# RWKV attention feeding a tanh-shrink MLP: two thirds of x @ w_in in blocks 6 to 11 as seven 128-column products, summed on VectorE

## The chip, the cores and the metric

The kernel runs on one core of one Trainium2 chip. The time is the device time of one execution in microseconds. The engines are named as the profile names them: PE (TensorE, with its weight loads as PEld), DVE (VectorE), ACT (ScalarE), POOL (GpSimd) and SP (SyncE, which only issues transfers). Everything is float32.

## The reference

```
def _attn_ref(r, k, v, w, u):              # r, k, v: (4, 8, 768, 48)
    for t in range(S):
        cur = einsum('bhd,bhe->bhde', u * k[t], v[t])
        y[t] = einsum('bhd,bhde->bhe', r[t], state + cur)
        state = w * state + einsum('bhd,bhe->bhde', k[t], v[t])
def _moe_ref(x, w_in, w_out):              # (3072, 384), (384, 2048), (2048, 384)
    h = x @ w_in
    g = h - tanh(h)
    return g @ w_out
```

The attention's output, laid out as 3072 tokens of 384, is x.

## The kernel before

**Tiling.** The 3072 tokens are 12 blocks of 256 (j = 0 to 11). The attention of a block is two units of 64 time steps and two batch rows each, 24 units in all; a unit ends with x transposed (384 channels on partitions in three slices of 128, kk = 0, 1, 2), written by ACT (`to_xt`, `to_rest`) and, for the channels that lie on the wrong partitions, by six small transfers that POOL issues (`fill`). d_ff is cut into 8 tiles of 256 columns. One block with one such tile is a tile of the MLP, T*j*.*n*: 96 in all. Blocks 0 to 5 go through d_ff in three passes (`PASSES`: tiles 0 and 1, then 2 and 3, then 4 to 7, each pass over all six blocks), blocks 6 to 11 in one.

**A tile.** `h` makes the 256 x 256 tile of x @ w_in transposed: two halves of 128 columns of d_ff, each three matmuls of 128 x 256 over the slices kk. A float32 matmul stands in the profile as two records, so this is 12 records. Then ACT reads h in PSUM three times (`s`, `th`, `tg`) and works on its own results twice (`sq`, `small`). DVE makes g = h - th (with h in PSUM), m (tg = s * tg) and copies m over g where the argument is small (`cp`, for the accuracy of h - tanh(h) near zero). Then POOL makes three sums of quarters of g (`sums_of_g`: one of 128x256, two of 128x128; on DVE for the last tiles of block 11), and PE the product with w_out (`products`), which is already done as seven products of 128 x 192 for eight, in two parts of 8 and 6 records, into four PSUM banks `p`. `mix` prepares the sums of w_out that it needs, on DVE, while blocks 2 to 5 run. At a block's end ACT and DVE put the four banks together (`collect`, and `gather` where an earlier pass left sums in `parts`), and POOL issues the stores. The last tile of block 11 has its product with w_out done plainly (`o`, `ALONE = 2`).

**What sets the order.** Nothing is scheduled while the program is built. `lay_out` lists all tasks with what they wait for, and `ORDER`, a string of task numbers, gives the order in which `written` emits them; each engine runs its own tasks in that order, and a wait stalls everything behind it on its engine. The costs and due times in the `add` calls are not used in this kernel. A PSUM tile named `h` is one of two buffers, so the h of a tile waits until s, th, tg and g of the tile two before have read theirs. g is one of five buffers and waits for the products of the tile five before. xt is one of eight buffers (`FIRST + 2`), reused after eight blocks.

Of the kernel before, what the change touches and what calls it, by code (L numbers as in the profile page):

```python
# [10 lines left out]
F32 = mybir.dt.float32  # L11
# [17 lines left out]
C = 128  # L29
# [10 lines left out]
EASED = 12  # L40

# [4 lines left out]
    "00010K2j2k2l2g2h2i0I2n2m2obXbX020F0L030J040605bXbY2r3536372p3332340A0G2t0B0C2s2vbXbY2y072w2z082x2u0U092+0M390N3V"  # L46
    "3D2_2q0O383A3B3H303W3X0P3F0V3I3T3J3C3K3E3S3U3G0Q3LbXbXbY3M0W3v3c310T3NbY3d3w3x0R3O3b3g3t3P3h3Q3s3u3f0S3Z3R3ibY8E"
    "0x3e3j0X3l3Y3a403k0Y4Q440Z8F0e3m4P4R0a454M41468G4N4O3n0b473z0D0c3_3o0E0d433p42bZ8Q160f483y3+3q4q0g8I494a4p4r0h4W"
    "4b0i4A4m8J4cbZ4B4S0j4d4n4o4X3r4C4V0k4T4U8R4w0m4D4Y5J4Z4K4E4e8M4L5Hba4f4J0l5K5L8S4G8H5G5I4g4I8K4H8Lba4v8T144h4+8V"
# [4 lines left out]
    "9L7M7b9M6v9U7j9V7k0H7D0y9K7F6wKM9e7GKNKO0z907a7c7e9f6x9NKPKR9W736y9C7H701M9Z7l6+717N0+K26_729g9D7O9X9i9a7d9Y7f9j"
    "Kt9b7P7mKv17KAK3K49O7QKBKwKx6z9P7h7gKsKu7RKaKb9s0_7SKS189h107n9R9Q9k9l9c197o111A7p129t7q9m1U1V1F9d1G7r1B1H7wA29n"
    "7u9w1C7v1I7yA31D7x9v7z9u9o9zA51f1gKC1W9x1X1J1hKD1i9pLG1KA6LHLIAG9y1N9q1OA4AHA91P9+9rAS9_KEA7ATA8AAAKKcA0AJABAVAN"
    "A11QKd1RACAI1SALAgAM1TAUAh1jAWAOAXAZAYAD1kAEAa1lAsK7AFAbLJAiAtKXAj1yAPAlLKLLAkAQLm1mAnLnLoAoARAvAwAuAzB4Ax1nAmB5"
# [1232 lines left out]
```

## Time and profile before

| | us |
|---|---|
| time, median of 3 runs (lowest, highest) | 579.02 (577.75, 583.08) |
| the profiled execution's own time | 576.89 |
| its span, first to last instruction | 575.2 |
| last h of block 11 ends on PE (start of the run of `p` that follows) | 556.85 |
| last instruction of DVE | 571.05 to 571.60 |

| tiles and units | engine | busy us of the span | share |
|---|---|---|---|
| all | PE | 562.6 | 98% |
| all | PE's weight loads | 481.1 | 84% |
| all | DVE | 430.3 | 75% |
| all | ACT | 404.3 | 70% |
| all | POOL | 202.8 | 35% |

The page gives per group of instructions the line, the engine, the shapes (partitions x elements), the count, the busy time and the mean of one in ns. In a view along the time each row has the start, the length, the engine and the line; a group of equal instructions is one row, with its count. Windows give the busy time of PE, PEld, DVE, ACT and POOL in a stretch, in that order, each with its number of records.

### The profile page before, as it was taken

How to read it: one execution, taken by the hardware profiler on the slowest of the kernel's cores; microseconds unless marked ns; L12 is line 12 of the kernel's file. 1: busy time of each engine (PE TensorE's matmuls, PEld its weight loads, DVE VectorE, ACT ScalarE, POOL GpSimd, SP SyncE). 2: the span in 40 equal slices, each digit the busy share in tenths (PEclk: the TensorE clock that was granted, in tenths of full speed). 3: DMA queues.
4: the chain of work that ended last, by engine and by line, in shares of the span. 5: the costliest groups of instructions: out<-in, count | busy, mean ns of one | idle time of the engine just before them, and what ended most of it. 6: DMA issues, size and time to landing. Idle time of an engine off the chain costs nothing.

```text
span 575.2 us, 14185 instructions
## 1 busy us (share of the span) xinstructions
PE 562.6 (98%) x5495; PEld 481.1 (84%) x5495; DVE 430.3 (75%) x720; ACT 404.3 (70%) x927; POOL 202.8 (35%) x366
## 2 busy tenths in 40 slices
PE   7989999999999999999999999999999999999997
PEld 4667777777677789999899899999999898999995
DVE  5899977989998877776897987487685774564445
ACT  2799999998778565545884875766785668666461
POOL 5101221300000236353345455182454263654430
PEclk9999999999999999999999999999999999999999
DMA  8987686535730000032344452442123010010011
GB/s 131 175 200 133 115 178 147 109 68 141 157 91 0 1 1 21 8 56 42 45 75 84 65 92 43 74 85 37 25 51 60 17 34 6 5 29 2 0 29 30
DMA packets 138399, 38.23 MB, mean 66 GB/s; under 512 B 130744, under 2 KB 132760, under 8 KB 138328
## 3 DMA queue, kind: packets, MB, share of 16 engines
q1 hardware_dynamic: 129996, 29.52, 28.5%
q0 software_dynamic: 4992, 6.99, 5.3%
q10 hardware_dynamic: 3340, 0.79, 0.9%
q8 instruction: 44, 0.72, 0.6%
q14 instruction: 27, 0.22, 0.1%
HBM read 31.46 MB, written 4.72 MB: 63 GB/s over the span
## 4 chain that ended last, share of the span: by engine, by line
PE 80%; DMA 1%; ACT 1%; POOL 0%; DVE 0%; issue 0%; POOLq 0%
PE h L217 39%; PE p L307 28%; PE o L254 7%; PE yk_ps L614 5%; DMA xt<-rest 1%; PE p L254 0%; ACT xt L773 0%; POOL xt L794 0%; ACT rest L773 0%; ACT st L188 0%; DVE last L265 0%; DVE state L800 0%; PE x_ps L614 0%; ACT kT L700 0%; POOLq L171 0%
## 5 line engine op out<-in xcount | busy, mean ns | idle before, releaser
L217 PE MATMUL h<-xt,w_in_sb 128*128 128x256 f32 x1152 | 269.0, 381 | 1.0 <-DVE w_in_sb L191 0.7
L217 PEld LDWEIGHTS h<-xt,w_in_sb 128*128 128x128 f32 x1152 | 214.8, 190 | 33.7 <-DVE w_in_sb L191 1.3
L290 POOL TENSOR_TENSOR sg<-g 128x256 f32<-128x256 f32 x69 | 56.9, 826 | 200.1 <-DVE g L246 145.6
L242 DVE TENSOR_TENSOR g<-h,th 128x512 f32<-128x512 f32 x96 | 65.8, 687 | 61.0 <-ACT tg L233 20.1
L244 DVE TENSOR_TENSOR tg<-s,tg 128x512 f32<-128x512 f32 x96 | 71.3, 746 | 32.9 <-ACT s L224 29.4
L229 ACT ACTIVATE s<-h 128x512 f32<-128x512 f32 x96 | 57.1, 595 | 54.1 <-PE h L217 39.5
L307 PE MATMUL p<-mixed,sg 128*128 128x192 f32 x426 | 93.0, 327 | 0.0
L246 DVE COPY_PREDICATED g<-small,tg 128x512 f32<-128x512 int32 x96 | 73.8, 778 | 12.6 <-ACT small L235 9.9
L231 ACT ACTIVATE th<-h 128x512 f32<-128x512 f32 x96 | 56.9, 594 | 35.0 <-PE h L217 34.7
L307 PEld LDWEIGHTS p<-mixed,sg 128*128 128x128 f32 x426 | 73.6, 190 | 1.4
L233 ACT ACTIVATE tg<-h 128x512 f32<-128x512 f32 x96 | 56.6, 592 | 22.9 <-DVE g L246 13.6
L307 PE MATMUL p<-w_out_sb,g 128*128 128x192 f32 x284 | 69.9, 328 | 0.0
L235 ACT ACTIVATE small<-s,smallb 128x512 f32<-128x512 f32 x96 | 68.5, 721 | 1.2
L254 PE MATMUL o<-w_out_sb,g 128*128 128x384 f32 x192 | 67.2, 489 | 0.1
L224 ACT ACTIVATE s<-s 128x512 f32<-128x512 f32 x96 | 60.1, 630 | 1.1
L794 POOL DMA_DIRECT2D xt<-rest x66 | 32.6, 498 | 66.2 <-ACT rest L773 65.4
L307 PEld LDWEIGHTS p<-w_out_sb,g 128*128 128x128 f32 x284 | 51.1, 190 | 2.7
L254 PEld LDWEIGHTS o<-w_out_sb,g 128*128 128x128 f32 x192 | 35.9, 190 | 19.4 <-issue 0.2
L712 ACT ACTIVATE at<-same,du 128x64 f32<-128x64 f32 x184 | 47.7, 339 | 3.9 <-DVE du L708 3.6
L292 POOL TENSOR_TENSOR sg<-sg,g 128x128 f32<-128x128 f32 x69 | 39.7, 579 | 3.6
L294 POOL TENSOR_TENSOR sg<-sg,g 128x128 f32<-128x128 f32 x69 | 37.7, 553 | 3.0
L307 PE MATMUL p<-w_out_sb,sg 128*128 128x192 f32 x142 | 34.8, 327 | 0.0
(130 smaller groups left out, 652.2 us busy)
## 6 DMA issues: line engine op xcount, KB each, us to landing
st<-in_moe_w_out_dram SPq DMA_DIRECT2D x8, 768.0 KB, 5.3
st<-in_moe_w_in_dram SPq DMA_DIRECT2D x16, 288.0 KB, 5.3
rt<-in_r_dram SPq DMA_DIRECT2D x46, 96.0 KB, 3.4
vt<-in_v_dram SPq DMA_DIRECT2D x46, 96.0 KB, 3.1
kt<-in_k_dram SPq DMA_DIRECT2D x44, 96.0 KB, 3.1
out_dram<-o POOLq DMA_DIRECT2D x44, 96.0 KB, 2.1
st<-in_moe_w_in_dram POOLq DMA_DIRECT2D x16, 96.0 KB, 6.0
parts<-in_k_dram SPq DMA_DIRECT2D x48, 32.0 KB, 2.0
```

The costliest lines, as they stand in the source:

```text
L217: self.nc.tensor.matmul(t.h2[:, z], self.w_in_sb[:, t.f // 2, kk, z * 128 : (z + 1) * 128], self.xts[t.j][:, kk].rearrange("p b t -> p (b ...
L224: A.activation(t.s, t.s, AF.Square, scale=G3)
L229: A.activation(out, t.h, AF.Arctan, scale=G2)
L231: A.activation(out, t.h, AF.Tanh)
L233: A.activation(out, t.h, AF.Tanh, scale=G1)
L235: A.activation(out, t.s, AF.Relu, bias=self.smallb, scale=-1.0)
L242: V.tensor_tensor(t.g, t.h, t.th, ALU.subtract)
L244: V.tensor_tensor(t.tg, t.s, t.tg, ALU.mult)
L246: V.copy_predicated(t.g, t.small.bitcast(I32), t.tg)
L254: self.nc.tensor.matmul(self.outs[i], t.g2[:, z, i * C : (i + 1) * C], self.w_out_sb[:, t.f + z, :], start=t.first and z == 0, stop=t.last ...
L290: add(t.s4[:, :2], g[:, 0::3], g[:, 1:2].to_broadcast([128, 2, C]), ALU.add)
L307: self.nc.tensor.matmul(ps[bank][:, half * n : (half + 1) * n], a, b, start=t.first and half == 0, stop=t.last, skip_group_check=True)
```

## The change

For blocks 6 to 11, all tiles but the last two of block 11 (`PLAIN = 4`), 46 tiles, the slices kk = 0 and 1 of x @ w_in are treated as a 2 x 2 by 2 x 2 product of 128 x 128 pieces and made with seven products for eight; the slice kk = 2 stays plain, as four products of the same size. `h_products` issues these 11 matmuls of 128 columns (22 records) in two parts: part 0, four matmuls into one buffer `h` (`ha`), part 1, seven into another (`hb`). So a tile takes both buffers, and each part waits for the reader of the part of the same kind one tile before.

`h_sums` puts h together in SBUF, in the tile of g: ACT copies one 128x128 quarter of `ha`, and DVE adds four times (128x256, 128x256, 128x128, 128x256), each with one operand in PSUM and one in SBUF. The first add reads `ha`, the other three `hb`. s, th, tg and g read h in SBUF after that; so g = h - th has both operands in SBUF. `g`'s buffer is taken by the ACT copy and not by the subtraction, so the wait for the products of the tile five before moves to that copy.

The sums of w_in (`mix_w`, twelve instructions, eight of 128x3x128 and four of 128x2x128) and of x (`mix_x`, four for each of the blocks 6 to 11, one of 128x256 and three of 128x128) are made by POOL. The first two sets of `mix_w` write over the slots of x of blocks 0 to 3 and wait for the last h of blocks 0 and 1, and of 2 and 3; the third writes into `parts` and waits for the gathers of blocks 3 to 5. `mix_x` waits for the block's fills and for the last h of the block two before (for block 6 and 7: gathers).

x no longer has eight rotating buffers but one array `held` of eight slots; blocks 8 to 11 use the slots of blocks 4 to 7 and wait for those blocks' last h.

`ORDER` is another string from its 458th task on: PE's order is the same until the second pass of block 5, at about 190 us.

```diff
+PLAIN = 4
-    "00010K2j2k2l2g2h2i0I2n2m2obXbX020F0L030J040605bXbY2r3536372p3332340A0G2t0B0C2s2vbXbY2y072w2z082x2u0U092+0M390N3V"
+    "00010K2j2k2l2g2h2i0I2n2m2ofhfh020F0L030J040605fhfi2r3536372p3332340A0G2t0B0C2s2vfhfi2y072w2z082x2u0U092+0M390N3V"
...
+    def h_products(self, t, part):
+
+        bank = self.ps_d.tile([128, 4, C], F32, name="h", tag="h")
+        setattr(t, "hb" if part else "ha", bank)
+        f, x = t.f // 2, self.xts[t.j]
+        w = self.w_in_sb[:, f].rearrange("p k (m t) -> p k m t", m=2)
+        a, b = self.mixed_w(f), self.mixed_x[t.j]
+        of = [[(2, w[:, 0, 0], x[:, 0, 0]), (1, a[:, 1], b[:, 2]), (0, w[:, 1, 0], x[:, 1, 0]), (0, w[:, 2, 0], x[:, 2, 0])],
+              [(0, a[:, 0], b[:, 0]), (1, a[:, 2], b[:, 3]), (1, w[:, 2, 1], x[:, 2, 1]), (2, a[:, 3], x[:, 1, 1]),
+               (2, w[:, 2, 0], x[:, 2, 1]), (3, w[:, 1, 1], b[:, 4]), (3, w[:, 2, 1], b[:, 1])]][part]
+        for n, (at, left, right) in enumerate(of):
+            self.nc.tensor.matmul(bank[:, at], left, right, start=n == 0, stop=n == len(of) - 1 or of[n + 1][0] != at,
+                                  skip_group_check=True)
+    def h_sums(self, t, n):
+
+        V = self.nc.vector
+        if n == 0:
+            t.g2 = self.gpool.tile([128, 2, self.d.NT], F32, name="g", tag="g")
+            t.h = t.g = t.g2.rearrange("p z t -> p (z t)")
+        q = t.g.rearrange("p (a t) -> p a t", a=4)
+        if n == 0:
+            self.nc.scalar.copy(q[:, 1], t.ha[:, 2])
+        elif n == 1:
+            V.tensor_tensor(q[:, 0::3], t.ha[:, :2], q[:, 1:2].to_broadcast([128, 2, C]), ALU.add)
+        elif n == 2:
+            V.tensor_tensor(q[:, 1:3], t.hb[:, :2], q[:, 3:4].to_broadcast([128, 2, C]), ALU.add)
+        elif n == 3:
+            V.tensor_tensor(q[:, 3], t.hb[:, 0], q[:, 2], ALU.add)
+        else:
+            V.tensor_tensor(q[:, 1:3], t.hb[:, 2:], q[:, 1:3], ALU.add)
+    def mix_w(self, f, x):
...
+        self.nc.gpsimd.tensor_tensor(s[:, :, out], a, b, op)
+    def mix_x(self, j, n):
...
+        self.nc.gpsimd.tensor_tensor(out, left, right, ALU.subtract)
-            t.g2 = self.gpool.tile([128, 2, self.d.NT], F32, name="g", tag="g")
-            t.g = t.g2.rearrange("p z t -> p (z t)")
+            if not hasattr(t, "ha"):
+                t.g2 = self.gpool.tile([128, 2, self.d.NT], F32, name="g", tag="g")
+                t.g = t.g2.rearrange("p z t -> p (z t)")
+    held = const.tile([128, FIRST + 2, NK, L, C], F32, name="held", tag="held")
...
+            for f, free in ((slice(0, 3), [last_h[0], last_h[1]]), (slice(3, 6), [last_h[2], last_h[3]]),
+                            (slice(6, 8), sum((gathered[j] for j in (3, 4, 5)), []))):
...
+                now = add("PE", .89, lambda: dense.h_products(t, 0), [x_ready[j], mixed_f[f // 2], b1.h] + before, due, steps=16)
+                x.made = add("ACT", .25, lambda: dense.h_sums(t, 0), [now, b5.o, b1.made])
+                first = add("DVE", .33, lambda: dense.h_sums(t, 1), [x.made])
+                users += [x.made, first]
+                before, users = bank(), h_users[-1]
+                x.h = add("PE", 1.55, lambda: dense.h_products(t, 1), [now] + before, due + 1.3, steps=28)
+                sums = [first]
+                for n in (2, 3, 4):
+                    sums.append(add("DVE", .2 if n == 3 else .33, lambda n=n: dense.h_sums(t, n), [x.h, sums[-1]]))
```

Three places in the order. In the rows, L343, L345 and L347 are the three sums of g in the changed kernel (L290, L292 and L294 before), L398 and L345 the stores after and before, L866 and L794 the fills, L264 is `mix_w`, L271 `mix_x`, L237 `h_products`, L222 a plain h (L217 before), L360 and L307 the products with w_out; `p_...` are its four banks.

First place: POOL while block 3 is in its third pass. Before, from the first sum of tile T3.4:

```order
L290 TENSOR_TENSOR sg<-g 128x256
L294 TENSOR_TENSOR sg<-sg,g 128x128
L292 TENSOR_TENSOR sg<-sg,g 128x128
L294 TENSOR_TENSOR sg<-sg,g 128x128
L345 DMA out_dram<-o 64x384
L290 TENSOR_TENSOR sg<-g 128x256
L292 TENSOR_TENSOR sg<-sg,g 128x128
L294 TENSOR_TENSOR sg<-sg,g 128x128
```

After, from the first `mix_w` of the second set, which waits for the last h of T3.7:

```order
L264 TENSOR_TENSOR held<-w_in_sb 128x3x128
L343 TENSOR_TENSOR sg<-g 128x256 x2
L345 TENSOR_TENSOR sg<-sg,g 128x128
L347 TENSOR_TENSOR sg<-sg,g 128x128
L264 TENSOR_TENSOR held<-held,w_in_sb 128x3x128
L343 TENSOR_TENSOR sg<-g 128x256
L264 TENSOR_TENSOR held<-w_in_sb 128x3x128
L398 DMA out_dram<-o 64x384 x2
L345 TENSOR_TENSOR sg<-sg,g 128x128
L347 TENSOR_TENSOR sg<-sg,g 128x128
L345 TENSOR_TENSOR sg<-sg,g 128x128
L347 TENSOR_TENSOR sg<-sg,g 128x128
```

Three sums of w_in now stand ahead of the last sums of g of T3.5 and T3.6 (the last four rows), and behind a wait for PE.

Second place: the first h of block 6, on PE. Before, the end of unit 14's outputs (`yk_ps`), products, and the h of T6.0 with the first half of the next (nine matmuls in one row); unit 13, which completes x of block 6, is further ahead, before the products of T4.6:

```order
L614 MATMUL yk_ps<-vt_123,kw_117 64x48 x16
L307 MATMUL p_2543<-mixed,sg 128x192
L307 MATMUL p_2541<-mixed,sg 128x192
L307 MATMUL p_2544<-w_out_sb,sg 128x192
L307 MATMUL p_2541<-w_out_sb,g 128x192
L307 MATMUL p_2542<-mixed,g 128x192
L307 MATMUL p_2543<-w_out_sb,g 128x192
L307 MATMUL p_2542<-mixed,sg 128x192
L217 MATMUL h<-xt,w_in_sb 128x256 x9
```

After, the last products of T4.7 and the two parts of T6.0:

```order
L360 MATMUL p_2447<-mixed,sg 128x192
L360 MATMUL p_2448<-w_out_sb,g 128x192
L360 MATMUL p_2448<-mixed,sg 128x192
L360 MATMUL p_2449<-w_out_sb,sg 128x192
L237 MATMUL h<-held,w_in_sb 128x128
L237 MATMUL h<-parts,held 128x128
L237 MATMUL h<-held,w_in_sb 128x128 x2
L237 MATMUL h<-parts,held 128x128 x2
L237 MATMUL h<-held,w_in_sb 128x128
L237 MATMUL h<-held 128x128
L237 MATMUL h<-held,w_in_sb 128x128
L237 MATMUL h<-parts,w_in_sb 128x128 x2
```

And on POOL the six fills of block 6 with what stands between them and that h:

```order
L866 DMA held<-rest 16x256 x6
L398 DMA out_dram<-o 64x384 x2
L343 TENSOR_TENSOR sg<-g 128x256
L345 TENSOR_TENSOR sg<-sg,g 128x128
L271 TENSOR_TENSOR parts<-held 128x256
L271 TENSOR_TENSOR parts<-held,parts 128x128
L271 TENSOR_TENSOR parts<-held 128x128
L271 TENSOR_TENSOR parts<-held,parts 128x128
```

The fills are now followed by four sums of x, for which the first h of the block waits. On PE, between unit 13's outputs and T6.0 stand the products of T4.5, T4.6 and T4.7 and the plain h of T5.7, and nothing else.

Third place: DVE in block 6. Before, in the collecting of a block (L335) beside the attention of a unit:

```order
L242 TENSOR_TENSOR g<-h,th 128x512
L688 STREAM_TRANSPOSE kT<-parts 128x512
L689 TENSOR_TENSOR kT<-kT,inverse 128x512
L335 TENSOR_TENSOR o<-u,p_2543 128x192
L815 TENSOR_TENSOR kw_118<-kt,w_down 128x8x48
L244 TENSOR_TENSOR tg<-s,tg 128x512
L246 COPY_PREDICATED g<-small,tg 128x512
L244 TENSOR_TENSOR tg<-s,tg 128x512
```

After (L250 to L256 are the four adds of `h_sums`, L297 is m, L299 cp, L388 the collecting, L392 the gather):

```order
L250 TENSOR_TENSOR g<-h,g 128x2x128
L388 TENSOR_TENSOR u<-e,p_2447 128x192
L388 TENSOR_TENSOR o<-u,p_2447 128x192
L388 TENSOR_TENSOR o<-u,p_2448 128x192
L388 TENSOR_TENSOR o<-e,p_2448 128x384
L392 TENSOR_TENSOR o<-o,parts 128x384
L388 TENSOR_TENSOR o<-o,p_2449 128x192
L252 TENSOR_TENSOR g<-h,g 128x256
L297 TENSOR_TENSOR tg<-s,tg 128x512
L392 TENSOR_TENSOR o<-o,parts 128x384
L254 TENSOR_TENSOR g<-h,g 128x128
L299 COPY_PREDICATED g<-small,tg 128x512
```

The adds of one tile stand between the instructions of the tiles before it; the first add of a tile frees its buffer `ha`, the last its buffer `hb`, for the PE's next tile.

More of the change, by code (lines that the diff above doesn't have):

```diff
@@ L90 @@
+    "eLe2eKeJeMdUdVeYepdWe4e3eNe5dodpdqe6e7e8dAd8dXdYdrdse9eAeOeZeaePeQeTd7eReSeUebeeedeseqecehefegeiejereteuevexewf7"
+    "f8fTfUeyfAf9fBe_ezf0e+f1f2f3fEfCf4fXfVfDfFfGfHfIfJfYfWfZfbfafcekenelemd9eof5f6fKfLfMfNfdfOfPfQfRfSfefgff"
 )
@@ L780, in given, with xt_at @@
                         copy(out[i * PAD : (i + 1) * PAD, z], y[to(i, z), i])
+            def xt_at(j):
+                return j if j < FIRST + 2 else j - 4
             def to_xt():
                 if slot == 0:
-                    dense.xts[j] = work.tile([128, NK, L, C], F32, name="xt", tag="xt", bufs=FIRST + 2)
+                    dense.xts[j] = held[:, xt_at(j)]
                 given(dense.xts[j][:, :, slot].rearrange("e p (z t) -> e z p t", z=2), y_ps[:, :, :NK])
@@ L840, in unit @@
                               [x.cp, x.diag, x.v, b1.xt, b1.rest, b1.add] + ([x.extra] if direct else [x.kw]), steps=96 if direct else 128)
-            x.xt = add("ACT", 1.2 if swap else .4, to_xt, [now, last_h.get(j - FIRST - 2) if slot == 0 else None])
+            x.xt = add("ACT", 1.2 if swap else .4, to_xt, [now, last_h[j - 4] if slot == 0 and j >= FIRST + 2 else None])
             if direct:
@@ L855, in lay_out, with by_seven, mixing_w, mixing_x @@
         tiles, stored, gathered = [], {}, {}
-        mixed = []
+        mixed, mixed_f, x_ready, h_users = [], {}, {}, []
+        def by_seven(j, f):
+            return j >= FIRST and not (j == d.NB - 1 and f >= d.NF - PLAIN)
+        def mixing_w():
+            plan.at = "mixing w"
+            for f, free in ((slice(0, 3), [last_h[0], last_h[1]]), (slice(3, 6), [last_h[2], last_h[3]]),
+                            (slice(6, 8), sum((gathered[j] for j in (3, 4, 5)), []))):
+                now = None
+                for x in range(4):
+                    now = add("POOL", .68 if f.stop == 8 else .95, lambda f=f, x=x: dense.mix_w(f, x), [now] + free)
+                for n in range(f.start, f.stop):
+                    mixed_f[n] = now
+        def mixing_x(j):
+            plan.at = "mixing x", j
+            now, ready = None, filled[j, "all"] + (gathered[j - 3 if j == FIRST else j - 2] if j < FIRST + 2 else [last_h[j - 2]])
+            for n in range(4):
+                now = add("POOL", .68 if n == 0 else .41, lambda n=n: dense.mix_x(j, n), [now] + ready)
+            x_ready[j] = now
         def mixing():
@@ L953, in lay_out @@
             done += part
-        for n in range(early, d.NU):
-            unit(n)
+        mixing_w()
         for j in range(FIRST, d.NB):
+            for n in range(len(units), min(L * (j + 4), d.NU)):
+                unit(n)
             ends = (d.NF,) if j < d.NB - 1 else (d.NF - ALONE, d.NF)
```

133 lines of the change are left out of this document (85 added, 48 removed).

## The prediction, as put on record before the changed kernel ran

> **What bounds the kernel now.** I read the page first, then PE's waits, then the chain in order of time.
>
> ```profile
> span 575.2 us, 14185 instructions
> PE 562.6 (98%) x5495; PEld 481.1 (84%) x5495; DVE 430.3 (75%) x720; ACT 404.3 (70%) x927; POOL 202.8 (35%) x366
> PE 80%; DMA 1%; ACT 1%; POOL 0%; DVE 0%; issue 0%; POOLq 0%
> L217 PE MATMUL h<-xt,w_in_sb 128*128 128x256 f32 x1152 | 269.0, 381 | 1.0 <-DVE w_in_sb L191 0.7
> ```
>
> PE is busy 98% and holds 80% of the chain that ended last; the x @ w_in group (L217) alone has 269 us and waited 1.0 us. The next rows are PE's only wait between 105 and 571 us, and the busy times of blocks 6 to 9 (columns: PE, PEld, DVE, ACT, POOL, then clock, transfers).
>
> ```profile
> PE h L217 <- DMA xt<-rest: 0.3, 1, 0.3
> 311.00:485.00 174.00, 174.00 (x1898) 158.33 (x1897) 126.41 (x211) 120.05 (x292) 79.91 (x134) 1.00 0.30 50
> ```
>
> The reader is to see that PE has no gap in these 174 us, at a granted clock of 1.00, and DVE has 174 - 126.4 = 47.6 us to spare. So fewer PE records shorten the kernel, one for one, as long as DVE, POOL and ACT deliver what PE waits for.
>
> The profiled execution took 576.89 us: span 575.2 and 1.7 around it. That is 2.1 us below the median, 579.02. I make the sum on the span and put the difference on the median.
>
> **PE: 22 short records for 12 long ones.**
>
> ```profile
> 121.51 2.59 PE h L217 x12
> 214.29 2.28 PE p L307 x14
> 15.08 0.60 PE L664 MATMUL x_ps<-ident,rt 128*128 128x128 f32 x4
> L664 PE MATMUL x_ps<-ident,rt 128*128 128x128 f32 x48 | 7.5, 280 | 1.7 <-DMA rt<-in_r_dram 1.3 <-DVE at L838 0.3
> 16.22 0.30 PEld L542 LDWEIGHTS h<-ident 128*128 128x128 f32 x2
> L217 PEld LDWEIGHTS h<-xt,w_in_sb 128*128 128x128 f32 x1152 | 214.8, 190 | 33.7 <-DVE w_in_sb L191 1.3
> ```
>
> The first two are rows of the chain: a tile's h is 12 records of 256 columns in 2.59 us, 0.216 each; a product with w_out is 14 of 192 in 2.28, 0.163 each. Both are 0.85 ns per column, each with a weight load of its own. At 128 columns that gives 0.109. The question is whether a load fits into 0.109. One load takes 0.19, but the row of two takes 0.30, so the next starts 0.11 after the first. And four 128-column matmuls with a load each (transposes) take 0.60; less one record's own 0.28 (the mean of their group) that is (0.60 - 0.28) / 3 = 0.11. I take 0.11: a tile 22 x 0.11 = 2.42 for 2.59, -0.17 us, and for 46 tiles **-7.6 us**. The ends: 0.109 gives -8.1; if records kept the 0.163 of the nearest plain products, 46 x (3.59 - 2.59) = +46. The gain is gone at 2.59 / 22 = 0.118. The evidence for 0.11 is short bursts near the start, hence a rival below.
>
> The Trainium skill (TensorE: Matmul & The Clock Gate, "Back-to-back issue gap") speaks against this change: in a stream of load and matmul pairs a 128-column matmul takes about 81 ns against 56 alone, so loads bind. Its ratio, 1.45, on 0.109 would make an estimated 0.158 per record, 3.48 per tile and +41 us. The transposes at 0.11 do not show it.
>
> **POOL in block 3's third pass.** Eight `mix_w` of three slices move into POOL's row there, of which three (with two stores) stand ahead of the sums of g of T3.5 and T3.6, behind a wait for T3.7's h.
>
> ```profile
> L290 POOL TENSOR_TENSOR sg<-g 128x256 f32<-128x256 f32 x69 | 56.9, 826 | 200.1 <-DVE g L246 145.6
> L292 POOL TENSOR_TENSOR sg<-sg,g 128x128 f32<-128x128 f32 x69 | 39.7, 579 | 3.6
> L294 POOL TENSOR_TENSOR sg<-sg,g 128x128 f32<-128x128 f32 x69 | 37.7, 553 | 3.0
> L345 POOL DMA_DIRECT2D out_dram<-o x44 | 24.1, 548 | 25.7 <-DVE o L339 19.1 <-DVE o L335 6.4
> ```
>
> Sums of 128 elements cost 0.57, of 256 0.83, so 384 are about 1.08. Between T3.7's h and the last sum of T3.5 the order gives POOL three `mix_w`, 3 x 1.08, three sums of 256, 3 x 0.83, six of 128, 6 x 0.57, and two stores, 2 x 0.55: 10.2 us. PE in that time has the h of T4.4 and T4.5 (5.18), T3.4's product (2.28) and the first half of T3.5's (1.30): 8.76. The second half waits about **+1.4**, and all of PE behind it. Bounds: 0, if POOL catches part of its sums beside DVE's waits, and +2.5, if two of its sums meet DVE as below (1.14 for 0.83, and more). The other `mix_w`, and the third set of four smaller ones, fall where POOL is often idle (200 us in all before L290); I cost them at nothing.
>
> **The first h of block 6.** It now waits for six fills and then four `mix_x`.
>
> ```profile
> 294.82 0.63 PE L614 MATMUL yk_ps<-vt,kw 64*64 64x48 f32 x32
> 311.04 2.32 PE L217 MATMUL h<-xt,w_in_sb 128*128 128x256 f32 x10
> 297.12 1.33 ACT L773 ACTIVATE xt<-yk_ps 64x192 f32<-64x192 f32 x4
> 298.46 0.91 ACT L773 ACTIVATE rest<-yk_ps 64x64 f32<-64x64 f32 x4
> 302.77 1.49 POOL L794 DMA_DIRECT2D xt<-rest  x3
> xt<-rest POOLq DMA_DIRECT2D x66, 16.0 KB, 2.2
> ```
>
> Before, 15.6 us lay between unit 13's outputs and that h. Now the order leaves PE three products and one plain h between: 3 x 2.28 + 2.59 = 9.43. The path: ACT 1.33 + 0.91, six fills 6 x 0.50 = 3.0, the landing 2.2 (stores and sums of g run meanwhile), `mix_x` 0.83 + 3 x 0.57 = 2.5, hand-offs 0.4: 10.4. PE waits **+1.0**; bounds 0 (ACT and fills overlap) and +2.5 (ACT starts 1.7 late, as in the rows above). Later blocks' fills come many tiles ahead; I cost their `mix_x` (24 us of POOL over 150) at nothing. The landing of a fill now matters there as it did at the 0.3 us wait above.
>
> **DVE in blocks 6 to 9.** This is the largest unknown. Per tile four adds: three of 256 elements, one of 128.
>
> ```profile
> L290 DVE TENSOR_TENSOR sg<-g 128x256 f32<-128x256 f32 x2 | 0.7, 413 | 0.0
> L292 DVE TENSOR_TENSOR sg<-sg,g 128x128 f32<-128x128 f32 x2 | 0.6, 283 | 0.0
> 222.08 0.34 DVE L335 TENSOR_TENSOR u<-e,p 128x192 f32<-128x192 f32 x1
> 222.45 0.35 DVE L335 TENSOR_TENSOR o<-u,p 128x192 f32<-128x192 f32 x1
> 204.51 0.55 DVE L267 TENSOR_TENSOR parts<-o,parts 128x384 f32<-128x384 f32 x1
> 204.98 0.55 DVE L316 TENSOR_TENSOR mixed<-mixed,w_out_sb 128x384 f32<-128x384 f32 x1
> ```
>
> Independent instructions start 0.08 before the last ends; one that needs the last starts 0.03 after (222.08 + 0.34 to 222.45). So a tile adds between 3 x 0.33 + 0.20 = 1.2 and 3 x 0.44 + 0.31 = 1.6 us. 32 tiles: 38 to 52 us, on 126.4 makes 165 to 179. PE's own time shrinks to 174 - 32 x 0.17 = 168.7. DVE is as full as PE, and whatever it has beyond PE's time, or loses in waits, PE loses too: 0 to +10.
>
> A second cost: g = h - th reads h in PSUM today and two tiles in SBUF after.
>
> ```profile
> 205.44 0.68 DVE L244 TENSOR_TENSOR tg<-s,tg 128x512 f32<-128x512 f32 x1
> 209.67 1.22 DVE L244 TENSOR_TENSOR tg<-s,tg 128x512 f32<-128x512 f32 x1
> 209.19 1.14 POOL L290 TENSOR_TENSOR sg<-g 128x256 f32<-128x256 f32 x1 [5.54 <-PE p L307]
> L242 DVE TENSOR_TENSOR g<-h,th 128x512 f32<-128x512 f32 x96 | 65.8, 687 | 61.0 <-ACT tg L233 20.1
> L244 DVE TENSOR_TENSOR tg<-s,tg 128x512 f32<-128x512 f32 x96 | 71.3, 746 | 32.9 <-ACT s L224 29.4
> ```
>
> m (L244, both inputs in SBUF) takes 0.68 alone and 1.22 beside a POOL sum; its mean is 0.746, that of g (one input in PSUM) 0.687. So g becomes like m: 32 x 0.06 = +1.9 us of DVE. The Trainium skill (SBUF, State Buffer, "Who interferes with whom") says the same of a DVE instruction with two SBUF inputs; the rows above agree.
>
> Where does PE then wait? Its next part 1 needs the three adds from `hb`, 0.33 + 0.20 + 0.33 and three hand-offs of 0.03: 0.95 us. Meanwhile PE makes the next part 0, 8 x 0.11 = 0.88, and one product, 2.28: 3.16. Alone on DVE the adds leave 2.2 to spare; behind a pair m and cp (0.68 + 0.76) still 0.8. Where a block is collected the order puts between a tile's first and last add the collecting, m, a gather and cp: about 5 x 0.35 + 2 x 0.55 + 0.75 + 0.55 + 0.76 = 4.9, with the adds 5.8, against 3.16 with one product or 5.44 with two beside it. That is a wait of 0.4 to 2.6, once per block; four blocks end in this stretch. I take 1.0 each, nearer the lower end because products often stand in pairs in PE's order: **+4**, a third of the 0 to +12 by the sums above. In blocks 10 and 11 DVE has no attention left, and I take nothing there but the tail.
>
> **Moved waits.** g's buffer is now taken by ACT's copy, some 2 us earlier than by g.
>
> ```profile
> DVE g L242 <- PE p L307: 6.7, 3, 3.5
> L326 ACT COPY e<-p 128x192 f32<-128x192 f32 x12 | 3.8, 314 | 6.8 <-PE p L307 6.8
> ```
>
> g waited three times for products, 6.7 us in all, which cost PE nothing; now s, th and tg of earlier tiles queue behind such a wait on ACT. Bounds 0 and 3 x 2 = +6 if all three fell into blocks 6 to 11 and PE starved for each; I take 0, since PE's products stand ahead of what ACT would feed. The copies are 46 x 0.31 = 14 us at most, on an ACT that is 70% busy: off the path. Slots of x that come back after four blocks, not eight, wait for an h made two blocks before they are written: nothing.
>
> **The tail.** Before, PE had five tiles' products left after the last h, 11.59 us; after, three, 6.84, then the plain tile.
>
> ```profile
> 556.85 11.59 PE p L307 x70
> 568.44 2.59 PE p L254 x8
> ```
>
> From T11.4's last add I count along ACT and DVE (s, th 1.1, g, m, cp to 3.9, T11.5's four adds to 5.3, its s and th, cp to 9.0, two sums 9.3) against PE's 1.55 + 5.18 + 2.28 = 9.0, and 0.3 again at T11.6: **+0.7**, bounds 0 and 1.4.
>
> **Sum.** -7.6 + 1.4 + 1.0 + 4.0 + 0.7 = -0.5: span 574.7, this execution 576.4, on the median **578.5**.
>
> **The rivals.** *The gain arrives whole.* For it: no wait of PE today, and adds that have 0.8 to 2.2 us to spare outside the collecting. Against: DVE at 165 of 168.7 or more. It gives -7.6 to -7.0, 571.4 to 572.0. Chance 0.20.
>
> *DVE becomes the bound in blocks 6 to 9* (the other side). It decides once DVE's work per tile passes PE's, that is at 168.7 - 126.4 = 42.3 us added, 1.32 per tile, between the 1.2 and the 1.6. At 1.6 and with contention on g, 126.4 + 52.2 + 1.9 - 168.7 = 11.8 stand in place of my 4: 586.3, and 588.9 with the upper ends of both POOL waits (+2.6). For it: the adds of one tile do hang on each other. Against: only those of one tile do, and others can stand between. Chance 0.20.
>
> *Loads bind the short records*, 0.118 or more each: from 0 to +46, some 600 at 0.14 (46 x (3.08 - 2.59) = +22). Chance 0.05.
>
> **How the numbers follow.** The forecast, waits that give back most, has 0.55, its own range 574 to 584. About 1% is what a measurement of this kernel can tell from no change: 573.2 to 584.8. Faster: the whole gain, 0.20. Same: 0.55. Slower: 0.20 + 0.05 = 0.25. The range reaches from the whole gain at the 0.109 end, 571.0, to the DVE rival's, 589.0.
>
> **What would show it.** A run of 22 records in the chain at 2.42 us, or 0.11 per record, shows the PE term; 2.6 or more the load rival. Waits of PE: a `p` on POOL's sums near T3.5, about 1.4; an `h` on `mix_x`, about 1.0, at T6.0. In blocks 6 to 9, DVE's busy time 165 to 179 less the time won, and PE's waits on DVE's adds summing to 4. The forecast is wrong if PE's gaps there are near 0, or if DVE is busy throughout and the stretch is longer than 174.

## The result, and the profile after

The changed kernel takes 599.66 us (median of 4 runs, 598.30 to 600.04) against 578.39 for the kernel before on the same chip: a ratio of 1.0352, 95% interval 1.0300 to 1.0404. It is 21 us slower, 11 us above the upper end of the forecast's range. The page of the profiled run (busy time of the engines, the shares of the chain that ended last, and the groups that answer to those shown of before):

```profile
span 597.9 us, 15412 instructions
PE 570.8 (95%) x5955; PEld 493.7 (83%) x5955; DVE 499.1 (83%) x904; ACT 417.7 (70%) x973; POOL 236.0 (39%) x402
PE 38%; DVE 28%; ACT 12%; SPq 7%; issue 6%; DMA 4%; POOL 4%; DVEq 0%; ACTq 0%; POOLq 0%
L237 PE MATMUL h<-held,w_in_sb 128*128 128x128 f32 x460 | 83.2, 279 | 0.9 <-DVE g L250 0.8
L343 POOL TENSOR_TENSOR sg<-g 128x256 f32<-128x256 f32 x69 | 56.2, 818 | 181.5 <-DVE g L299 100.4
```

PE's share of the chain went from 80% to 38%; DVE holds 28% now, and was busy 499 us for 430. The stretch from 311 to 560 us, of the kernel before and then of the changed one (columns as in the prediction); it is blocks 6 to 11 before, and blocks 6 to 10 with part of 11 after:

```profile
311.00:560.00 249.00, 249.00 (x2295) 228.02 (x2294) 164.35 (x269) 166.92 (x378) 116.73 (x195) 1.00 0.22 39
```

```profile
311.00:560.00 249.00, 238.00 (x2784) 227.66 (x2783) 222.05 (x439) 171.38 (x420) 133.29 (x214) 0.99 0.26 45
```

DVE was busy 66% of this stretch and is busy 89%. PE had no gap in it and has 11 us of gaps, though DVE is still not full. In four parts (blocks 6 to 9 before), the changed kernel:

```profile
311.00:350.00 39.00, 34.93 (x416) 32.93 (x415) 34.48 (x71) 23.48 (x59) 21.39 (x32) 0.98 0.44 71
350.00:391.00 41.00, 39.65 (x449) 37.98 (x448) 36.20 (x73) 27.40 (x71) 18.75 (x34) 0.98 0.24 44
391.00:438.00 47.00, 45.86 (x559) 43.73 (x558) 41.87 (x84) 32.45 (x81) 26.70 (x45) 1.00 0.33 54
438.00:485.00 47.00, 44.76 (x554) 42.85 (x553) 45.93 (x90) 33.66 (x83) 21.56 (x32) 1.00 0.30 50
```

Of these parts DVE fills only the last (98%). PE's gaps are widest in the first (4.1 us), where DVE is busy 88%. What PE waited for in the changed kernel between 105 and 570 us:

```profile
PE p L360 <- POOL sg L345: 3.5, 5, 1.7
PE h L237 <- DVE g L256: 3.4, 7, 0.8
PE yk_ps L683 <- DVE state L872: 2.0, 3, 0.8
PE p L360 <- POOL sg L347: 1.8, 2, 1.5
PE h L237 <- DVE g L250: 1.5, 3, 0.7
PE p L360 <- POOL sg L343: 0.7, 1, 0.7
```

Three sorts of wait, none longer than 1.7 us: products for POOL's sums of g (6.0 us), parts of h for DVE's adds (4.9), the attention for DVE (2.0). They are about half of what is to be explained: 21 us of loss, and PE's shorter records, which give 5.6 where nothing holds them up (below). A matmul's record is drawn 0.28 us long (the mean of L237 above), but the next can start 0.11 after it, so up to 0.17 us of every wait passes for busy time. PE's busy time has risen from 562.6 to 570.8 us although its records are shorter (about 2 us of that are the clock, see the last section). How a wait comes about, in the chain of the changed kernel in order of time (start, length, what):

```profile
399.58 0.69 DVE tg L297
400.27 0.20 DVE g L254
400.47 0.47 DVE state L872
400.94 0.60 DVE g L295
401.54 0.34 DVE g L256
401.87 0.63 DVE rT L757
402.52 0.69 DVE rT L758
403.21 0.65 DVE g L299
403.86 0.30 DVE g L250
404.17 1.12 DVE g L295
405.29 1.15 DVE tg L297
...
406.53 0.80 DVE g L299
407.33 0.31 DVE g L252
...
407.67 0.30 DVE g L254
...
407.99 0.44 DVE g L256
...
409.05 0.71 ACT small L287
409.76 0.16 ACT g L248
409.94 0.43 DVE g L250
410.42 1.16 PE h L237 x8
```

For 9 us the chain runs along DVE's own order: adds of one tile (L250 to L256), g, m and cp of others (L295, L297, L299), the attention's work (L757, L758, L872), each behind the last. Its last two steps go over ACT: ACT's queue comes to the copy of a quarter of the next tile's h (L248), DVE's add L250 follows and frees `ha`, and PE gets its next part of h at 410.4. No single instruction is late; the queue is. Two of them, g and m at 404 and 405, are stretched to 1.1 us (0.75 and 0.76 by their groups' means). On POOL, a sum of g and the first sums of x of a block (L271, the first of them 1.16 long for a mean of 0.83) ran beside them.

The terms of the prediction that can be read off directly: short records run at 0.11 us. A whole tile of 22 in the chain of the changed kernel:

```profile
320.19 2.45 PE h L237 x22
```

and the adds take 0.42 and 0.29, g 0.747 for 0.687, the copy on ACT 0.255, the sums of w_in of three slices on POOL 1.16 to 1.28 by their groups where 1.08 had been put:

```profile
L250 DVE TENSOR_TENSOR g<-h,g 128x256 f32<-128x256 f32 x46 | 19.1, 415 | 6.1 <-ACT g L248 5.9
L254 DVE TENSOR_TENSOR g<-h,g 128x128 f32<-128x128 f32 x46 | 13.3, 289 | 1.1
L295 DVE TENSOR_TENSOR g<-g,th 128x512 f32<-128x512 f32 x46 | 34.3, 747 | 8.9 <-ACT th L283 3.6 <-ACT tg L285 3.4 <-ACT s L281 1.9
L248 ACT COPY g<-h 128x128 f32<-128x128 f32 x46 | 11.7, 255 | 33.6 <-PE h L237 29.2 <-PE p L360 4.3
L264 POOL TENSOR_TENSOR held<-w_in_sb 128x384 f32<-128x384 f32 x4 | 5.1, 1284 | 9.8 <-PE h L222 9.8
```

So each term's instructions cost about what was forecast. What they did to PE was not.

### The profile page after: what moved, and what is told of

Same layout as the page of the kernel before. It is cut to its first block, busy times and chain, and to the rows that moved or that the text cites. A ratio compares the mean times of both kernels' runs of the same rounds, so it can differ in the third digit from the quotient of the medians.

```text
span 597.9 us, 15412 instructions
## 1 busy us (share of the span) xinstructions
PE 570.8 (95%) x5955; PEld 493.7 (83%) x5955; DVE 499.1 (83%) x904; ACT 417.7 (70%) x973; POOL 236.0 (39%) x402
## 4 chain that ended last, share of the span: by engine, by line
PE 38%; DVE 28%; ACT 12%; SPq 7%; issue 6%; DMA 4%; POOL 4%; DVEq 0%; ACTq 0%; POOLq 0%
PE h L222 12%; PE p L360 8%; PE o L307 7%; PE h L237 7%; SPq L752 5%; DVE g L299 4%; DVE tg L297 4%; DVE g L295 4%; ACT at L781 2%; PE yk_ps L683 2%; ACT held L842 2%; SPq L721 2%; DVE g L256 2%; ACT tg L285 1%; DVE g L252 1%
## 5 line engine op out<-in xcount | busy, mean ns | idle before, releaser
L222 PE MATMUL h<-held,w_in_sb 128*128 128x256 f32 x600 | 138.8, 382 | 0.3
L222 PEld LDWEIGHTS h<-held,w_in_sb 128*128 128x128 f32 x600 | 112.0, 190 | 22.1 <-DVE g L295 2.7
L343 POOL TENSOR_TENSOR sg<-g 128x256 f32<-128x256 f32 x69 | 56.2, 818 | 181.5 <-DVE g L299 100.4
L360 PE MATMUL p<-mixed,sg 128*128 128x192 f32 x426 | 92.7, 330 | 4.7 <-POOL sg L345 3.5
L237 PE MATMUL h<-held,w_in_sb 128*128 128x128 f32 x460 | 83.2, 279 | 0.9 <-DVE g L250 0.8
L299 DVE COPY_PREDICATED g<-small,tg 128x512 f32<-128x512 int32 x96 | 76.1, 796 | 6.5 <-ACT small L287 3.4
L360 PEld LDWEIGHTS p<-mixed,sg 128*128 128x128 f32 x426 | 71.8, 190 | 8.1 <-POOL sg L345 5.9
L297 DVE TENSOR_TENSOR tg<-s,tg 128x512 f32<-128x512 f32 x96 | 72.9, 764 | 6.4 <-ACT s L276 4.3
L360 PE MATMUL p<-w_out_sb,g 128*128 128x192 f32 x284 | 70.5, 330 | 0.4 <-DVE o L388 0.4
L237 PEld LDWEIGHTS h<-held,w_in_sb 128*128 128x128 f32 x460 | 67.2, 193 | 2.3 <-DVE g L250 1.9
L307 PE MATMUL o<-w_out_sb,g 128*128 128x384 f32 x192 | 66.9, 489 | 0.0
L866 POOL DMA_DIRECT2D held<-rest x66 | 32.0, 491 | 61.8 <-ACT rest L842 61.5
L295 DVE TENSOR_TENSOR g<-h,th 128x512 f32<-128x512 f32 x50 | 34.3, 687 | 26.1 <-ACT tg L285 8.8
L307 PEld LDWEIGHTS o<-w_out_sb,g 128*128 128x128 f32 x192 | 36.0, 190 | 19.6
L360 PEld LDWEIGHTS p<-w_out_sb,g 128*128 128x128 f32 x284 | 48.1, 191 | 1.8 <-DVE o L388 0.7
L347 POOL TENSOR_TENSOR sg<-sg,g 128x128 f32<-128x128 f32 x69 | 42.2, 615 | 3.9
L285 ACT ACTIVATE tg<-h 128x512 f32<-128x512 f32 x50 | 29.6, 592 | 19.4 <-PE h L222 12.8
L345 POOL TENSOR_TENSOR sg<-sg,g 128x128 f32<-128x128 f32 x69 | 40.6, 590 | 3.6
L295 DVE TENSOR_TENSOR g<-g,th 128x512 f32<-128x512 f32 x46 | 34.3, 747 | 8.9 <-ACT th L283 3.6
```

What stands on the lines that cost most here:

```text
L222: self.nc.tensor.matmul(t.h2[:, z], self.w_in_sb[:, t.f // 2, kk, z * 128 : (z + 1) * 128], self.xts[t.j][:, kk].rearrange("p b t -> p (b ...
L237: self.nc.tensor.matmul(bank[:, at], left, right, start=n == 0, stop=n == len(of) - 1 or of[n + 1][0] != at, skip_group_check=True)
L295: V.tensor_tensor(t.g, t.h, t.th, ALU.subtract)
L297: V.tensor_tensor(t.tg, t.s, t.tg, ALU.mult)
L299: V.copy_predicated(t.g, t.small.bitcast(I32), t.tg)
L307: self.nc.tensor.matmul(self.outs[i], t.g2[:, z, i * C : (i + 1) * C], self.w_out_sb[:, t.f + z, :], start=t.first and z == 0, stop=t.last ...
```

## The experiments

Theory A: DVE's added time (the adds) is what PE waits for. Theory B: POOL's added time (the sums of w_in and x) pushes the sums of g. Theory C: the new order costs by itself. Each ratio is against the kernel before on the run's own chip (577.7 to 578.6 us); differences between runs are taken from the times as they stand. Where the adds are cut, the five buffers of g are five fixed tiles; what that does by itself was not tried.

### The adds, cut to two columns

```diff
-            V.tensor_tensor(q[:, 0::3], t.ha[:, :2], q[:, 1:2].to_broadcast([128, 2, C]), ALU.add)
+            V.tensor_tensor(q[:, 0, :2], t.ha[:, 0, :2], q[:, 1, :2], ALU.add)
...
-            V.tensor_tensor(q[:, 1:3], t.hb[:, 2:], q[:, 1:3], ALU.add)
+            V.tensor_tensor(q[:, 1, :2], t.hb[:, 2, :2], q[:, 1, :2], ALU.add)
```

> The four DVE adds per seven-product tile are cut to 128x2 (h is left unmade, so g and the output are not the reference's), everything else of the changed kernel stays: its order, the 22 short records, the ACT copies, the sums of w_in and x on POOL. The five g buffers are five fixed tiles here. Theory A, the adds' own DVE time (499 us busy for 430) is what PE waits for: most of the 21 us come back, 573 to 582. Rival B, POOL's new work: 597 or more. Rival C, the new order of all engines whatever they carry: 593 or more.

588.92 us, ratio 1.0187 (1.0170 to 1.0204). 10.7 us came back, half of the loss. Between the figures of A and of its rivals: the adds are a half, not the whole.

### The sums of w_in and x, cut to two columns

```diff
-        self.nc.gpsimd.tensor_tensor(s[:, :, out], a, b, op)
+        self.nc.gpsimd.tensor_tensor(s[:, :, out, :2], a[:, :, :2], b[:, :, :2], op)
...
-        self.nc.gpsimd.tensor_tensor(out, left, right, ALU.subtract)
+        self.nc.gpsimd.tensor_tensor(out[..., :2], left[..., :2], right[..., :2], ALU.subtract)
```

> The sums of w_in and of x on POOL are cut to two columns (their products are then not the reference's), all else as changed, the DVE adds whole. Theory A: 597 to 600. Rival B (POOL pushes the sums of g that PE waits for, 6.3 us of PE's waits): 580 to 593. Rival C: 597 to 600. I expect a part only: 594 to 598.

590.89 us, ratio 1.0229 (1.0206 to 1.0252): 8.8 us came back, more than the 6.0 that PE's waits for POOL add up to, and more than expected of it.

### Both cuts

> Both cuts at once: adds on DVE and sums of w_in and x on POOL are two columns wide, the order, the short records and the ACT copies stay. If the added work is the whole cause (A with B) the gain of PE alone is left: 571 to 573. Under C, the order itself costs: 580 or more, and the excess over 572 is its price.

580.89 us, ratio 1.0048 (1.0031 to 1.0065). 18.8 us came back, 10.7 + 8.8 = 19.5 by the two runs apart: they add up within 1 us. 580.9 is at the edge of C: something else is left.

### Short records alone, in the old order

```diff
+        if t.j >= FIRST and not (t.j == d.NB - 1 and t.f >= d.NF - LATE):
+            n = 5 + z
+            for i in range(n):
+                kk, half = i % d.NK, i * 2 // n
+                self.nc.tensor.matmul(t.h2[:, z, half * 128 : (half + 1) * 128],
+                                      self.w_in_sb[:, t.f // 2, kk, z * 128 : (z + 1) * 128], self.xts[t.j][:, kk, half],
...
+            return
```

> The kernel before with its own order, and for the same 46 tiles 11 matmuls of 128 columns for six of 256 (h is not the reference's there); no adds, no copies, no sums of w_in or x. If short records run at 0.111 us as in the changed kernel's chain, PE's gain is 46 x (2.59 - 2.45) = 6.4 us and shows whole: 571 to 573. If PE's gain was never there, 577 to 580.

572.98 us, ratio 0.9902 (0.9886 to 0.9919): PE's gain is real, 5.6 us of the expected 6.4, and arrives whole when nothing else changes. In the chain of that run 32 short records stand without a gap, 0.1116 each:

```profile
505.06 3.57 PE h L220 x32
```

Against it, both cuts have 580.89 - 572.98 = 7.9 us left.

### Which of POOL's sums, and work or place

The first of the next two runs has only the line of `mix_w` of the second experiment; the second cuts nothing and moves eight task numbers in `ORDER`.

> Only the twelve sums of w_in on POOL are cut to two columns (products with them are not the reference's); the sums of x stay whole. Both cut gave 590.9 for 599.7. If the 8.8 us come from the sums of w_in (waits of PE for POOL's sums of g at 267 to 276 and at 317 us, 4.4 us together), 592 to 596; if from the sums of x, one set per block, 598 to 600.

594.03 us, ratio 1.0272 (1.0230 to 1.0315): the sums of w_in are 5.6 of the 8.8 us, those of x about 3.1.

> Nothing is cut. The eight sums of w_in of the first two sets move in POOL's order alone: the first set ahead of the wait for T3.7's h, into POOL's idle 9.8 us before 260.8, the second set behind the sums of g of T4.4, into its idle 8.5 us before 290.9. If their cost is their place in POOL's queue, as the prediction had it: 594 to 596.5, as with the sums of w_in cut. If POOL's work costs by contending with DVE wherever it stands: 598 to 600.

594.99 us, ratio 1.0280 (1.0236 to 1.0323), 4.7 us of those 5.6, with all the work still done. Their place in POOL's queue was the cost. On POOL, the changed kernel and then the moved one:

```profile
250.11 0.86 POOL L347 TENSOR_TENSOR sg<-sg,g 128x128 f32<-128x128 f32 x2
260.77 0.99 POOL L264 TENSOR_TENSOR held<-w_in_sb 128x384 f32<-128x384 f32 x1 [9.80 <-PE h L222]
261.73 1.87 POOL L343 TENSOR_TENSOR sg<-g 128x256 f32<-128x256 f32 x2
```

```profile
251.86 0.87 POOL L347 TENSOR_TENSOR sg<-sg,g 128x128 f32<-128x128 f32 x2
252.69 1.00 POOL L264 TENSOR_TENSOR held<-w_in_sb 128x384 f32<-128x384 f32 x1
253.77 0.99 POOL L264 TENSOR_TENSOR held<-held,w_in_sb 128x384 f32<-128x384 f32 x1
```

In the changed kernel POOL stood 9.8 us at a sum of w_in that waited for T3.7's h, with the four sums of the first set behind it, which could have run, and then did all of it among the sums of g. Moved, the four of the first set run in that gap.

### The same load off DVE in another place

```diff
-            V.copy_predicated(t.g, t.small.bitcast(I32), t.tg)
+            n = 2 if hasattr(t, "ha") else 2 * self.d.NT
+            V.copy_predicated(t.g[:, :n], t.small[:, :n].bitcast(I32), t.tg[:, :n])
```

> The adds stay whole; in the 46 tiles the copy of m over g (cp, DVE) is cut to two columns (g is not the reference's where the argument is small). Cutting the adds took 46 x (1.54 - 0.3) = 57 us off DVE and gave 10.8 us. If what costs is DVE's load (it is busy 93% of 311 to 560 us), 46 x 0.7 = 32 us off it in another place give their share, 5 to 8 us: 591 to 595. If it is the length of the loop from PE's h through the adds back to the next h, cp is not in it: 598 to 600.

590.49 us, ratio 1.0217 (1.0160 to 1.0274): 9.2 us for 24 us less on DVE (475.0 busy for 499.1), a little more than expected. (DVE is busy 89% of 311 to 560 us by the window above, not 93%.) cp is not between PE's h and its next h, so it is DVE's load that costs. cp does stand ahead of POOL's sums of g, so a part of the 9.2 came that way, by PE's waits the smaller one: between 105 and 570 us those for POOL's sums of g went from 6.0 to 4.4 us, while those for the adds went from 4.9 to none that the view lists, with 0.8 put down to cp (L300 of that run) in their place.

### ACT's copies

On top of both cuts:

```diff
-            self.nc.scalar.copy(q[:, 1], t.ha[:, 2])
+            self.nc.scalar.copy(q[:, 1, :2], t.ha[:, 2, :2])
```

> As the kernel with both cuts (580.9), and ACT's copy of a quarter of h cut to two columns too. Against the short records in the old order (573.0) that one has 7.9 us left. If they come from the copies on ACT: 574 to 577. If from the new order: 579 to 581.

581.87 us, ratio 1.0059 (1.0034 to 1.0085), no better than 580.89. With both cuts made the copies are hidden. With the adds whole, where one stands in the chain shown above, they were not tried.

### The old work in the new order

`by_seven` gives false for every tile and `mix_w` does nothing; `ORDER` is the changed kernel's without the tasks that are gone, and 67 of PE's h tasks stand later, behind the readers of the buffer that they need.

> The work of the kernel before (no seven products of h, no adds, no sums of w_in and x), in the order of the changed kernel; only PE's h stands later where it would have overrun the two buffers of a plain h. With both cuts 580.9 was left against 573.0 for short records in the old order. If those 7.9 us are the new order's own price: 584 to 588. If they came with the rest of the new tile (what is left of the adds, h in SBUF): 577 to 581.

623.75 us, ratio 1.0781 (1.0739 to 1.0822), far outside both. The order can't be had with the old tile: PE waits 26.1 us there for g = h - th (L292 of that run), which is the last to read a whole tile's h, where the changed tile's adds free a buffer early. So this run says nothing on the 7.9 us.

### The change in the old order

The task numbers of the order before, with each tile's copy and adds put in, for blocks 10 and 11 (14 tiles), 9 to 11 (22) and 6 to 11 (46). In the first two the sums of x also wait for the gathers of blocks 4 and 5.

> The seven products for blocks 10 and 11 alone (14 tiles), in the order of the kernel before: copies and adds put in front of the first reader of each h, the sums of w_in into POOL's idle stretches between 336 and 479 us. DVE is busy 45 of 86 us there. By the measured 5.6 us for 46 tiles PE gains 1.7, the last block's end may give 0.7 back: 576.5 to 578.5. If the adds' place in the chain h, adds, ACT, g costs even where DVE is free: 580 or more.

598.69 us, ratio 1.0353 (1.0327 to 1.0380).

> As the last one, with block 9 as well (22 tiles). Between 438 and 485 us DVE was busy 29 of 47 us; eight tiles' adds are 8 x 1.54 = 12.3 more, 41 of 46. PE gains 2.7. If DVE's load decides and 90% is too much: 578 to 581; if not: 575.5 to 577.5.

614.26 us, ratio 1.0641 (1.0617 to 1.0666).

> The whole change (46 tiles) in the order of the kernel before, copies and adds put in by the same rule, the sums of w_in in POOL's idle stretches from 236 us on. If the new order is a price of its own (7.9 us) and the sums of w_in cost only by their place (4.7): 599.7 - 12.6 = 585 to 590. If the new order is what makes the adds bearable: 600 or more.

663.86 us, ratio 1.1482 (1.1456 to 1.1507). The first and the third came out on the side of their second branch (580 or more, 600 or more), far beyond it; the second missed both its ranges. Each lost 1.5 to 1.9 us per tile against the kernel before. In the first, while DVE is busy only 60% of 485 to 597 us, PE waits for the adds all the same:

```profile
PE h L234 <- DVE g L247: 6.8, 7, 2.1
PE h L234 <- DVE g L253: 2.9, 7, 0.8
PE p L357 <- DVE o L385: 2.3, 3, 1.3
```

(L247 is the first add of a tile, L253 the last.) The new order is therefore no burden laid on the change but most of what makes it bearable: +21 us with it, +86 with the adds put into the old order by this rule.

### The last 7.9 us, and what a load on DVE does where nothing waits for it

The first run joins the cuts of adds, sums and cp. The second is short records in the old order, and behind each of the 46 tiles' cp:

```diff
...
+                a, w = self.extra, self.w_out_sb[:, 0, :256]
+                V.tensor_tensor(a, w, w, ALU.add)
+                V.tensor_tensor(a, a, w, ALU.add)
+                V.tensor_tensor(a[:, :128], a[:, :128], w[:, :128], ALU.add)
+                V.tensor_tensor(a, a, w, ALU.add)
```

> The kernel with both cuts (580.9, DVE busy 453 us), and cp cut to two columns in the 46 tiles as well: some 28 us less on DVE, under the 433 of short records in the old order. If the 7.9 us left are DVE's load: 573 to 576.5. If they are the new order's own: 579 to 581.

578.35 us, ratio 1.0009 (0.9992 to 1.0025): between the two. 2.5 of the 7.9 us go with DVE's load (426 us busy, less than the 433 of the old order); 5.4 (6.2 by the two ratios, since the chips differ) stay with the new order or the new tile's waits. Part of these 5.4 is there before block 6, where the work is the same as before but for stubs on POOL. The window from 200 to 311 us of that run, against 111.00 of 111 for the kernel before:

```profile
200.00:311.00 111.00, 109.86 (x811) 98.72 (x810) 82.59 (x139) 66.13 (x135) 56.62 (x95) 1.00 0.18 32
```

> Short records in the old order (573.0), and behind each of the 46 tiles' cp four adds on DVE of the sizes of the change (three of 256, one of 128 elements), on a scratch tile that nothing waits for. If DVE's load alone costs: 583 to 595. If it needs the loop h, adds, ACT, next h: 573 to 577.

611.53 us, ratio 1.0587 (1.0560 to 1.0614): 38.5 us more than without those adds, for 86 us more on DVE (1.9 per tile, more than the change's 1.54). No other engine waits for them; they only stand in DVE's queue. PE's waits there:

```profile
PE h L220 <- DVE g L250: 14.7, 9, 2.7
PE p L324 <- DVE o L352: 6.4, 4, 3.1
```

(L250 is g = h - th, which frees h; L352 the collecting.) A load on DVE costs PE without any loop through the adds. Part of the 38.5 is PE's clock: at the mean of 0.989 granted in that run, 0.011 x 609 = 6.7 us (the last section).

> As the seven products for blocks 10 and 11 in the old order (598.7), but each tile's copy and first add stand right behind part 0 and its other adds right behind part 1 in the order, ahead of whatever ACT and DVE did there before. If the adds' late place was what cost: 576 to 583. If the loop costs wherever they stand: 590 or more.

598.19 us, ratio 1.0357 (1.0325 to 1.0390), the same as with the later place (598.69). So it isn't the adds' own place that cost 20 us in blocks 10 and 11. What exactly does (the two buffers that one tile now takes, s, th and tg a microsecond later, or the queue behind the adds) was not separated.

### DVE's load moved to POOL

```diff
-            eased = across_by == "DVE" and EASED <= n < early
+            eased = across_by == "DVE" and n >= EASED
```

on top of the moved sums of w_in.

> The kernel with the sums of w_in moved (595.0), and four instructions of each unit from the 13th on (kw, rk twice, the state's decay, 2.4 us per unit) go from DVE to POOL. If DVE's load decides: some 25 us off it give 587 to 592. If POOL, with 45 us more, pushes the sums of g: 596 or more.

614.20 us, ratio 1.0616 (1.0580 to 1.0653), the side of POOL, 19 us more than without. DVE fell only to 486 us busy, POOL rose from 235 to 279. POOL is no place to put it in this order.

No version that does all the work beat the kernel before; short records alone did, by leaving out what makes them h.

## Why the prediction was wrong, point by point

The four runs that nest into one another give the sum, in us:

| step | time | difference | forecast |
|---|---|---|---|
| kernel before | 578.6 | | |
| short records alone, old order | 572.98 | -5.6 | -7.6 |
| new order and tile, adds and sums cut | 580.89 | +7.9 | 0 |
| with the sums of w_in and x whole | 588.92 | +8.0 | +2.4 |
| with the adds whole: the changed kernel | 599.66 | +10.7 | +4.0 and 0.7 |

Against the forecast, the adds with the tail came out 6.0 us dearer, POOL 5.6, the order with the new tile 7.9, and PE's gain 2.0 smaller. No single step makes the miss: one was wrong in kind (DVE's capacity rule), one was left out (the order), and two were mis-sized (POOL and PE's gain).

**PE's records: right.** 0.111 to 0.112 for the forecast 0.11; 46 x 22 x 0.0016 = 1.6 us of the missing 2.0 are that difference, so the step was the right one and slightly mis-sized. (Its arithmetic was off too: 46 x 0.17 is 7.8, not 7.6, and 0.109 per record would give 8.8, not 8.1.) The rule of the Trainium skill that was weighed there (TensorE: Matmul & The Clock Gate, "Back-to-back issue gap") would have made an estimated 0.158 of it: 32 records without a gap at 0.1116 do not show it.

**The tail: nearly right.** The forecast had two waits of 0.3, which make 0.6, not its 0.7; the profile has gaps of 0.26 for T11.6's sums on DVE and 0.38 after it. From the start of T11.5's part 1 to the plain tile's product lie 14.7 us (574.92 to 589.58) against 13.6 of PE's own by the forecast's prices (1.55 + 5.18 + 3 x 2.28): 1.1 us. The chain of that time runs along DVE and ACT, as the forecast counted it.

**POOL: the step "Eight `mix_w` ... ahead of the sums of g", and "I cost them at nothing".** The mechanism was right, and moving the eight sums gave 4.7 us against the forecast 1.4. The size was off twice: they ran at 1.16 to 1.28 us, not 1.08 (1.00 in the gap of the moved run, most of it with DVE idle), and the five that do not stand ahead of the sums of T3.5 and T3.6 were costed at nothing, though one of them stood ahead of POOL's sums at 317 us, where PE waited 1.7. The first h of block 6, for which 1.0 had been put, waited 0.2; the 3.1 us of the sums of x were put at nothing elsewhere (with 24 us of POOL's time, which by the forecast's own prices are 5 x 2.5 = 13). Of these, 2.2 us show as gaps of PE between 311 and 560 us (9.0 with the sums of x whole, 6.8 with them cut, those of w_in cut in both runs).

**DVE: the step that failed.** The prediction said of DVE that "whatever it has beyond PE's time, or loses in waits, PE loses too: 0 to +10", found the adds hidden outside the collecting because they "leave 2.2 to spare", and put one wait of 1.0 per block. The load came as forecast (1.54 us per tile of 1.2 to 1.6, g 0.06 slower), and the capacity rule did not hold: PE had 11 us of gaps in the stretch above, and more in short waits, while DVE still had 11% of its time free. The runs show in its place that the price begins before DVE is full. By DVE's busy time (on the page of each run): from 426 to 453 us 2.5 us of time, from 461 to 499 us 10.7, the last 24 of them alone 9.2 where cp is what was cut. And 86 us on DVE that nothing waits for cost 38.5. The rival "DVE becomes the bound" had the right engine and side, and its condition was met: the measured 1.54 us per tile lies above its threshold of 1.32, as did the middle of the forecast's own 1.2 to 1.6. Put into its sum, 126.4 + 32 x 1.54 + 1.9 - 168.7 gives 8.9 us, near the 10.7 that the adds cost. That nearness is in part luck, for it is the price of a DVE without free time over the four blocks, and DVE had 9% free in the four parts above, with PE's widest gaps not where it was fullest. Where PE waits, though, DVE is full for some microseconds: it has no gap to speak of in the 9 us of the chain shown above, and is busy 4.9 of the 5 us from 346 to 351 (rows in the last section). A sum over blocks sets the free time of one place against the load of another.

**The new order: left out of the sum.** The prediction costed the order itself at nothing. 5.4 us remain with DVE's load back at the old level; 1.1 us of gaps of PE in the window before block 6 are part of it. The other 2.5 of the 7.9 went with cp. Whether the rest belongs to the order or to the longer way from PE's h to g (copy, adds, then ACT) stays open: the old work in this order makes PE wait for g, which is a cost of its own, and the new work in the old order is dearer still.

## What to carry to other kernels

Where PE waits for nothing and every other engine works in a fixed order, the spare time of those engines need not be spare: here it was what let each wait end before PE got there. Price an addition to such an engine by the microsecond added (here 0.1 us of time for one at 75% load, 0.3 to 0.4 at 80%, and 0.45 in an order not made for it, of which about 0.08 was PE's clock), not only by what exceeds the engine's capacity. A saving on PE of 0.12 us per tile can't pay for 1.5 us on the next engine. And work with no deadline, such as sums of weights, belongs ahead of a queue's long waits: an instruction that waits at the head holds up those behind that could run.

## What the runs showed of the hardware that was not expected

After a few short waits PE's clock itself can fall. In the changed kernel PE waited 0.84 us at 346 us and 0.65 at 348, and then 14 records of 128 columns took 3.16 us in the chain, 0.226 each, twice the usual:

```profile
348.20 3.16 PE h L237 x14
```

The granted clock (the third number from the end) by windows, changed kernel:

```profile
346.00:348.00 2.00, 1.16 (x64) 1.02 (x64) 1.93 (x6) 0.79 (x3) 0.00 (x0) 1.00 0.40 49
348.00:351.00 3.00, 2.80 (x14) 2.83 (x14) 2.97 (x7) 0.63 (x1) 2.03 (x4) 0.56 0.53 100
351.00:354.00 3.00, 3.00 (x77) 2.72 (x77) 3.00 (x7) 1.22 (x4) 0.11 (x1) 0.87 0.33 47
```

The Trainium skill (TensorE: Matmul & The Clock Gate, "HAM oscillation — how this bites in real kernels") gives as its abstract rule that PE should have no idle gap above about 3.4 us; here the longest wait of PE in the three microseconds ahead of the fall was 0.84 us. Nor does the length of one wait decide. After a wait of 1.7 us at 317 us the changed kernel kept a clock of 1.00, and with cp cut the same wait of 1.7 us was followed by 3.4 us at 0.50 (320.0 to 323.4). What decides is not shown. Over the whole run it is little: a mean clock of 0.997, or 0.003 x 598 = 1.8 us. Runs with more waits lost more: 0.989 in the run with idle adds, and 0.966 in the whole change in the old order, which is 0.034 x 665.5 = 22.6 of its 86 us. But it is not a matter of the waits' sum alone: the change in blocks 10 and 11 lost 20 us and was profiled at 1.00.
